# q of the first FFN tile loaded in runs of four tokens per partition

## The chip, the cores and the metric

The kernel runs on one core of one Trainium2 chip. The metric is the device time of one execution in microseconds (us). The engines are named as the profile names them: PE (TensorE, the matmuls), DVE (VectorE), ACT (ScalarE), POOL (GpSimd) and SP (SyncE). Repeated executions of one kernel mostly agree within 1% here, and each has a granted TensorE clock in its record (1.0 is full speed). A ratio is the mean time of one kernel's fast runs over that of the other's of the same rounds on the same chip, so it is not quite the ratio of the medians quoted beside it; the bracket behind it is its 95% interval.

## The reference

A recurrent attention (each head has a decay `gamma`) is followed by a gated FFN over all 3072 tokens:

```
B, H, S, D = 4, 8, 768, 64
gamma = 1.0 - 2.0 ** (-5.0 - np.arange(H))
for t in range(S):
    state = gamma * state + einsum('bhd,bhe->bhde', k[:, :, t], v[:, :, t])
    y[:, :, t] = (1 / sqrt(D)) * einsum('bhd,bhde->bhe', q[:, :, t], state)
x = y.transpose(0, 2, 1, 3).reshape(B * S, H * D)          # 3072 x 512
out = (sigmoid(x @ w_gate) * (x @ w_val)) @ w_out            # d_ff = 1536
```

## The kernel before

The tokens are cut into 24 chunks of 128, six for each batch, and into six FFN tiles of four chunks. An "up" group of the FFN computes 128 of the 1536 hidden columns of a tile (8 matmuls), a "down" group half the sum for 128 output rows (6 matmuls). The attention of tile t+1 is woven into the FFN of tile t. For each chunk, k and q are loaded, transposed on PE (chunks 0 to 11) and multiplied to scores; DVE masks these; PE adds the part inside the chunk ("intra") and the part from the state ("inter") in the PSUM tile `y`; DVE multiplies `y` by the decay table `taby` into the FFN's input `xT`. `y` has one buffer (pool `pa`, `bufs=1`), so a chunk's `y` starts only after the `xT` of the chunk before it.

Nearly all loads are issued by POOL (GpSimd), which also does some arithmetic. These are the parts, with cuts marked:

```python
    def load_kq(g):
        kn[g] = ld.tile([C, H, D], BF16, tag="kn", name="kn")
        qn[g] = ld.tile([C, H, D], BF16, tag="qn", name="qn")
        nc.gpsimd.dma_start(out=kn[g], in_=src(k, g))
        nc.gpsimd.dma_start(out=qn[g], in_=src(q, g))
    def load_chunk(g):
        load_kq(g)
        load_v(g, nc.gpsimd)
    ...
    def extend_taby():           # columns 384..767 = columns 0..383 times gamma^384
        nc.gpsimd.tensor_tensor(taby[:, :, 384:768], taby[:, :, 0:384],
                                gup.unsqueeze(2).to_broadcast([128, NP, 384]), op=ALU.mult)
    ...
    def y_out(g):
        c = g % NCH              # ... xT of chunk g reads columns c*128 .. of taby
        nc.vector.tensor_tensor(xT[g // 4][:, :, col:col + C], y[g], taby[:, :, c * C:(c + 1) * C], op=ALU.mult)
    ...
    keep_on(36)                  # 36 dummy matmuls
    transposes(0)
    make_taby(slice(256, 384))
    extend_taby()                # early
    ... load_gate_val(3..5), load_chunk(4), load_out(0..3), load_chunk(5..7)
    ... attention of chunks 0 to 3, with the first FFN groups of tile 0
    for t in range(NT):
        groups, steps, place = ups(t) + downs(t), [], []
        if t == 0:
            groups = groups[4:]
            steps = [lambda: step_t(4), lambda: step_s(4), lambda: step_y(4), lambda: step_t(5), lambda: step_s(5),
                     lambda: step_t(6), lambda: step_y(5, 6), lambda: step_t(7), lambda: step_y(6, 7)]
            place = [4, 5, 7, 9, 10, 11, 12, 13, 14]
        ...
        if t + 2 < NT:
            for g in range(4 * t + 8, 4 * t + 12):
                load_chunk(g)    # for t == 0: chunks 8 to 11, ahead of all groups of tile 0
        for i, group in enumerate(groups):
            ...
            group()
            for p, step in zip(place, steps):
                if p == i:
                    step()
```

## Time and profile before

| | before |
|---|---|
| median of 4 runs (range) | 240.16 us (239.56 to 241.09) |
| span of the profiled run | 238.1 us, PE busy 227.8 |
| FFN tile 0 / tile 1 entered by PE | 27.9 / 57.7 us |
| granted clock | 1.00 from its first record (6.0 us) on |

From the page of the kernel before come the PE row and the clock row (the span in 40 slices of about 6 us, each digit the tenths of a slice) and the engines' shares of the chain of work that ended last:

```profile
PE   7798999999999999999999999999999999999993
PEclk9999999999999999999999999999999999999999
...
PE 88%; POOL 6%; issue 2%; ACT 2%; DVE 1%; ACTq 0%; POOLq 0%; DVEq 0%
```

The rows have no hole after the fourth slice, and the chain is PE for 88% of the span. So any stretch in which PE waits is added to the time, and nothing that another engine saves shortens it unless PE waits for it.

### The profile page before, as it was taken

What the parts mean: (1) busy time and instruction counts of PE and PEld (TensorE: products, weight loads), DVE (VectorE), ACT (ScalarE), POOL (GpSimd) and SP (SyncE); (2) the same over time, 40 slices, a digit from 0 to 9 for tenths busy, and PEclk for the clock granted to TensorE, in tenths of its full rate; (3) what the DMA queues carried; (4) which work ended last, traced back from release to release, by engine and by line L of the source; (5) the groups of instructions that cost most, each with busy time, mean ns of one, the idle gap of its engine ahead of it and who ended that gap; (6) DMA issues with size and microseconds to landing.
All of it is one profiled execution on the core that took longest, in us unless ns stands there. A gap on an engine that the chain in (4) does not pass through costs nothing.

```text
span 238.1 us, 4313 instructions
## 1 busy us (share of the span) xinstructions
PE 227.8 (96%) x1716; PEld 118.9 (50%) x1742; DVE 102.0 (43%) x172; ACT 90.8 (38%) x169; POOL 95.9 (40%) x114
## 2 busy tenths in 40 slices
PE   7798999999999999999999999999999999999993
PEld 7565644555655554444554445444444554444441
DVE  3467446355545631256641346641346641243300
ACT  7764334425545431234333243223334321334221
POOL 8999874687889346994111001111000000000000
PEclk9999999999999999999999999999999999999999
DMA  7999999999999999999972361012100012100022
GB/s 131 192 189 188 195 205 200 189 212 230 233 169 139 92 138 163 263 175 156 159 110 88 91 104 29 3 45 89 47 0 0 3 44 88 47 0 0 0 88 88
DMA packets 77267, 27.27 MB, mean 115 GB/s; under 512 B 65024, under 2 KB 72704, under 8 KB 77248
## 3 DMA queue, kind: packets, MB, share of 16 engines
q0 software_dynamic: 57616, 16.78, 70.6%
q1 hardware_dynamic: 19632, 10.23, 21.6%
q8 instruction: 13, 0.21, 0.4%
q14 instruction: 6, 0.05, 0.1%
HBM read 28.31 MB, written 6.29 MB: 145 GB/s over the span
## 4 chain that ended last, share of the span: by engine, by line
PE 88%; POOL 6%; issue 2%; ACT 2%; DVE 1%; ACTq 0%; POOLq 0%; DVEq 0%
PE ff L250 49%; PE ff L281 26%; PE sA L168 3%; PE y L204 2%; PE z L190 2%; PE y L180 2%; PE tp L146 2%; POOL vs L158 1%; POOL kn L67 1%; POOL vf L62 1%; POOL qn L68 1%; ACT qkT L148 1%; PE ff L264 1%; ACT ob L286 1%; PE ff L293 1%
## 5 line engine op out<-in xcount | busy, mean ns | idle before, releaser
L255 DVE TENSOR_TENSOR hT<-gs,ff 128x512 bf16<-128x512 f32 (+1 forms) x72 | 48.6, 676 | 75.5 <-PE ff L250 73.9
L250 PE MATMUL ff<-xT,wg 128*128 128x512 bf16 (+1 forms) x276 | 71.5, 375 | 0.9 <-DVE xT L212 0.3
L250 PE MATMUL ff<-xT,wv 128*128 128x512 bf16 (+1 forms) x282 | 71.9, 375 | 0.4
L254 ACT ACTIVATE gs<-ff 128x512 f32<-128x512 f32 (+1 forms) x72 | 42.3, 588 | 68.8 <-PE ff L250 68.3
L281 PE MATMUL ff<-wo,hT 128*128 128x512 bf16 x280 | 65.0, 380 | 0.6 <-issue 0.2
L250 PEld LDWEIGHTS <-wv 128*128 128x128 bf16 x288 | 28.2, 98 | 32.7
L281 PEld LDWEIGHTS <-hT 128*128 128x128 bf16 x288 | 27.0, 98 | 31.6
L250 PEld LDWEIGHTS <-wg 128*128 128x128 bf16 x288 | 26.7, 98 | 30.2 <-issue 0.8
L158 POOL TENSOR_TENSOR vs<-vf,tabv 128x512 bf16<-128x512 f32 x18 | 18.6, 1048 | 47.1 <-PE y L204 42.1
L286 ACT COPY ob<-ff 128x512 f32<-128x512 f32 x24 | 14.0, 585 | 54.3 <-PE ff L281 49.1
L212 DVE TENSOR_TENSOR xT<-y,taby 128x512 bf16<-128x512 f32 x24 | 16.4, 685 | 20.1 <-PE y L204 20.0
L62 POOL DMA_DIRECT2D vf<-in_v_dram x23 | 20.7, 902 | 9.4 <-DMA kn<-in_k_dram 4.7
L173 DVE TENSOR_TENSOR stA<-sA,causal 128x512 bf16<-128x512 f32 x24 | 16.5, 687 | 18.6 <-PE sB L168 18.5
L67 POOL DMA_DIRECT2D kn<-in_k_dram x23 | 20.9, 907 | 7.0 <-DMA qn<-in_q_dram 4.4
L68 POOL DMA_DIRECT2D qn<-in_q_dram x23 | 20.4, 887 | 4.3 <-DMA wo<-in_moe_w_out_dram 2.3
L198 ACT CAST zbd<-z 64x256 bf16<-64x256 f32 x40 | 14.6, 366 | 13.6 <-PE z L190 13.2
L174 DVE TENSOR_TENSOR stB<-sB,causal 128x512 bf16<-128x512 f32 x24 | 16.3, 681 | 0.0
L148 ACT ACTIVATE qkT<-tp 128x1024 bf16<-128x1024 bf16 x12 | 12.3, 1024 | 5.1 <-PE tp L146 5.1
L293 PE MATMUL ff<-ident 128*128 128x128 bf16 x110 | 9.5, 251 | 2.6 <-POOL ident masks.py:199 1.6
L204 PE MATMUL y<-stA,vs 128*64 128x128 bf16 x96 | 9.7, 222 | 0.0
L293 PEld LDWEIGHTS <-ident 128*128 128x128 bf16 x110 | 8.0, 114 | 3.2 <-POOL ident masks.py:199 1.6
L204 PE MATMUL y<-stB,vs 128*64 128x128 bf16 x96 | 9.5, 221 | 0.0
(48 smaller groups left out, 112.9 us busy)
## 6 DMA issues: line engine op xcount, KB each, us to landing
out_dram<-ob SPq DMA_DIRECT2D x24, 256.0 KB, 2.0
vf<-in_v_dram POOLq DMA_DIRECT2D x23, 256.0 KB, 8.6
kn<-in_k_dram POOLq DMA_DIRECT2D x23, 128.0 KB, 8.4
qn<-in_q_dram POOLq DMA_DIRECT2D x23, 128.0 KB, 8.6
wg<-in_moe_w_gate_dram POOLq DMA_DIRECT2D x6, 256.0 KB, 5.8
wv<-in_moe_w_val_dram POOLq DMA_DIRECT2D x6, 256.0 KB, 6.6
wo<-in_moe_w_out_dram POOLq DMA_DIRECT2D x4, 384.0 KB, 11.0
kf<-in_k_dram SPq DMA_DIRECT2D x1, 256.0 KB, 3.4
```

Source lines behind the costliest of these rows:

```text
L62: eng.dma_start(out=vf[g], in_=src(v, g))
L67: nc.gpsimd.dma_start(out=kn[g], in_=src(k, g))
L68: nc.gpsimd.dma_start(out=qn[g], in_=src(q, g))
L158: eng.tensor_tensor(vs[g], vf[g], tabv[:, g % NCH, :].unsqueeze(2).to_broadcast([C, H, D]), op=ALU.mult)
L173: nc.vector.tensor_tensor(stA[g], sc[g][0], causal4, op=ALU.mult)
L204: nc.tensor.matmul(y[g][i * D:(i + 1) * D, p, :], vs[g][:, 2 * p + i, :], st[:, p, :], start=(first and p == 0), stop=True, skip_group_che ...
L212: nc.vector.tensor_tensor(xT[g // 4][:, :, col:col + C], y[g], taby[:, :, c * C:(c + 1) * C], op=ALU.mult)
L250: nc.tensor.matmul(u[:, lo:hi], w[:, kk, n1 * 128:(n1 + 1) * 128], xT[t][:, kk, lo:hi], start=(kk == 0), stop=(kk == KT - 1))
L254: nc.scalar.activation(gs[:, lo:hi], ps[0][:, lo:hi], AX.Sigmoid)
L255: nc.vector.tensor_tensor(hT[t][:, n1, lo:hi], gs[:, lo:hi], ps[1][:, lo:hi], op=ALU.mult)
L281: nc.tensor.matmul(o, hT[t][:, n1, sm * 128:(sm + 1) * 128], wo[:, n1, :], start=(n1 == 0), stop=(n1 == NFF - 1))
L293: nc.tensor.matmul(u[:, :128], ident, ident, start=True, stop=True)
```

## The change

The intent is to read q for the first tile (tokens 0 to 511) with one load instead of four. Each partition takes four consecutive tokens, so that the runs in memory are longer and there are fewer loads at the start. The tokens of a chunk of tile 0 are then in the order "j, p" (token 4p + j) through the mask, the decay table, the FFN and the stores, which put them in order again. The decay table of tile 0 becomes a table of its own (`taby0`). The table in plain order, `taby`, which chunk 4 and later chunks need, is now made from it during tile 0 by three ACT copies and one POOL multiply.

```diff
     def load_kq(g):
         kn[g] = ld.tile([C, H, D], BF16, tag="kn", name="kn")
-        qn[g] = ld.tile([C, H, D], BF16, tag="qn", name="qn")
         nc.gpsimd.dma_start(out=kn[g], in_=src(k, g))
-        nc.gpsimd.dma_start(out=qn[g], in_=src(q, g))
+        if g >= 4:
+            qn[g] = ld.tile([C, H, D], BF16, tag="qn", name="qn")
+            nc.gpsimd.dma_start(out=qn[g], in_=src(q, g))
...
-    nc.sync.dma_start(out=qf, in_=src(q, 0))
...
+    q0 = const.tile([128, H, 4 * D], BF16, name="q0")
+    nc.gpsimd.dma_start(out=q0, in_=q[0, :, 0:512, :].rearrange("h (p j) d -> p h (j d)", j=4))
...                                             # iota, mask and table of tile 0 in the order (j, p)
-    def extend_taby():
-        nc.gpsimd.tensor_tensor(taby[:, :, 384:768], taby[:, :, 0:384],
-                                gup.unsqueeze(2).to_broadcast([128, NP, 384]), op=ALU.mult)
+    def by_384(out, in_):
+        nc.gpsimd.tensor_tensor(out, in_, gup.unsqueeze(2).to_broadcast([128, NP, in_.shape[2]]), op=ALU.mult)
+    def taby_in_order(c):
+        nc.scalar.copy(taby[:, :, c * C:(c + 1) * C].rearrange("x n (p j) -> x n p j", j=4),
+                       taby0[:, :, c * C:(c + 1) * C].rearrange("x n (j p) -> x n p j", j=4))
...                                             # transposes_q0: 32 transposes of 64 columns, two copies
-    transposes(0)
-    make_taby(slice(256, 384))
-    extend_taby()
+    transposes_k(0)
+    keep_on(10)
+    transposes_q0()
+    make_taby0(slice(256, 384))
+    by_384(taby0[:, :, 384:512], taby0[:, :, 0:128])
...
-    transposes(3)
-    keep_on(16)
+    transposes_k(3)
...                                             # stores of tile 0: four of 64 KB for one of 256 KB
             place = [4, 5, 7, 9, 10, 11, 12, 13, 14]
+            steps += [lambda c=c: taby_in_order(c) for c in range(3)]
+            steps += [lambda: by_384(taby[:, :, 384:768], taby[:, :, 0:384])]
+            place += [0, 1, 2, 3]
```

More of the change, by code (lines that the diff above doesn't have):

```diff
@@ L89 @@
     kf = const.tile([C, H, D], F32, name="kf")
-    qf = const.tile([C, H, D], F32, name="qf")
     nc.sync.dma_start(out=kf, in_=src(k, 0))
-    nc.sync.dma_start(out=qf, in_=src(q, 0))
     nc.scalar.preload_act_table(AX.Exp)
     load_v(0, nc.sync)
+    q0 = const.tile([128, H, 4 * D], BF16, name="q0")
+    nc.gpsimd.dma_start(out=q0, in_=q[0, :, 0:512, :].rearrange("h (p j) d -> p h (j d)", j=4))
+    q0T = const.tile([128, NP, 4, 128], BF16, name="q0T")
     tokv = const.tile([128, NCH], I32, name="tokv")
@@ L99, with causal_mask @@
     toky = const.tile([128, 384], I32, name="toky")
-    nc.gpsimd.iota(toky, pattern=[[1, 384]], base=0, channel_multiplier=0)
+    nc.gpsimd.iota(toky, pattern=[[C, 3], [1, 4], [4, 32]], base=0, channel_multiplier=0)
     load_chunk(1)
-    causal = const.tile([128, 128], F32, name="causal")
-    nc.gpsimd.memset(causal, 1.0)
-    nc.gpsimd.affine_select(causal, causal, pattern=[[1, 128]], base=0, channel_multiplier=-1,
-                            compare_op=ALU.is_ge, fill=0.0)
+    def causal_mask(name, pattern):
+        m = const.tile([128, 128], F32, name=name)
+        nc.gpsimd.memset(m, 1.0)
+        nc.gpsimd.affine_select(m, m, pattern=pattern, base=0, channel_multiplier=-1,
+                                compare_op=ALU.is_ge, fill=0.0)
+        return m.unsqueeze(1).to_broadcast([128, NP, 128])
+    causal0 = causal_mask("causal0", [[1, 4], [4, 32]])
     load_chunk(2)
@@ L123, with make_taby0 @@
     taby = const.tile([128, NP, S], F32, name="taby")
-    def make_taby(cols):
+    taby0 = const.tile([128, NP, 512], F32, name="taby0")
+    def make_taby0(cols):
         for p in range(NP):
-            nc.scalar.activation(taby[:, p, cols], toky[:, cols], AX.Exp, scale=lgp[:, p:p + 1], bias=lsc)
-    def extend_taby():
-        nc.gpsimd.tensor_tensor(taby[:, :, 384:768], taby[:, :, 0:384],
-                                gup.unsqueeze(2).to_broadcast([128, NP, 384]), op=ALU.mult)
-    causal4 = causal.unsqueeze(1).to_broadcast([128, NP, 128])
+            nc.scalar.activation(taby0[:, p, cols], toky[:, cols], AX.Exp, scale=lgp[:, p:p + 1], bias=lsc)
+    def by_384(out, in_):
[3 more added lines that the diff above has]
+                       taby0[:, :, c * C:(c + 1) * C].rearrange("x n (j p) -> x n p j", j=4))
     xT, vs, qkT, sc, stA, stB, y = {}, {}, {}, {}, {}, {}, {}
@@ L140, in pair, with transposes_q0, transposes_k, q_of @@
         return t[:, 2 * p:2 * p + 2, :].rearrange("s h d -> s (h d)")
+    def transposes_q0():
+        for i in range(2):
+            tq = pf.tile([128, 2, 4, 128], BF16, tag="ff", name="tq")
+            for p in range(2):
+                for j in range(4):
+                    for k in range(2):
+                        nc.tensor.transpose(tq[k * D:(k + 1) * D, p, j, :],
+                                            q0[:, 2 * (2 * i + p) + k, j * D:(j + 1) * D], ident)
+            if i:
+                nc.vector.tensor_copy(q0T[:, 2:4], tq)
+            else:
+                nc.scalar.activation(q0T[:, 0:2], tq, AX.Copy)
+    def transposes_k(g):
+        tp = pa.tile([128, 2 * NP, C], BF16, tag="tp", name="tp")
+        for p in range(NP):
+            nc.tensor.transpose(tp[:, p, :], pair(kn[g], p), ident)
+        qkT[g] = at.tile([128, 2 * NP, C], BF16, tag="qkT", name="qkT", bufs=3)
+        nc.scalar.activation(qkT[g][:, 0:NP], tp[:, 0:NP], AX.Copy)
+    def q_of(g, rows, p):
+        if g < 4:
+            return q0T[rows, p, :, g * 32:(g + 1) * 32]
+        return qkT[g][rows, NP + p, :]
     def transposes(g):
@@ L167, in scores @@
                 half = slice(i * D, (i + 1) * D)
-                nc.tensor.matmul(sc[g][i][:, p, :], t[half, p, :], t[half, NP + p, :], start=True, stop=True)
+                nc.tensor.matmul(sc[g][i][:, p, :], t[half, p, :], q_of(g, half, p), start=True, stop=True)
     def masks(g):
@@ L172, in masks @@
         stB[g] = at.tile([128, NP, C], BF16, tag="stB", name="stB")
-        nc.vector.tensor_tensor(stA[g], sc[g][0], causal4, op=ALU.mult)
-        nc.vector.tensor_tensor(stB[g], sc[g][1], causal4, op=ALU.mult)
+        mask = causal0 if g < 4 else causal4
+        nc.vector.tensor_tensor(stA[g], sc[g][0], mask, op=ALU.mult)
+        nc.vector.tensor_tensor(stB[g], sc[g][1], mask, op=ALU.mult)
     def inter(g):
@@ L179, in inter @@
             for p in range(NP):
-                nc.tensor.matmul(y[g][:, p, :], zbd[(g - 1) % 2][:, p, :], qkT[g][:, NP + p, :],
+                nc.tensor.matmul(y[g][:, p, :], zbd[(g - 1) % 2][:, p, :], q_of(g, slice(0, 128), p),
                                  start=(p == 0), stop=False, skip_group_check=True)
@@ L211, in y_out @@
         col = (g % 4) * C
-        nc.vector.tensor_tensor(xT[g // 4][:, :, col:col + C], y[g], taby[:, :, c * C:(c + 1) * C], op=ALU.mult)
+        tab = taby0 if g < 4 else taby
+        nc.vector.tensor_tensor(xT[g // 4][:, :, col:col + C], y[g], tab[:, :, c * C:(c + 1) * C], op=ALU.mult)
     def step_t(g):
@@ L286, in down @@
         nc.scalar.copy(ob, o)
-        row = t * 512 + sm * 128
-        nc.sync.dma_start(out=out[row:row + 128, :], in_=ob)
+        rows = out[t * 512 + sm * 128:t * 512 + (sm + 1) * 128, :]
+        if t > 0:
+            nc.sync.dma_start(out=rows, in_=ob)
+        else:
+            for j in range(4):
+                nc.sync.dma_start(out=rows.rearrange("(p j) d -> j p d", j=4)[j], in_=ob[j * 32:(j + 1) * 32, :])
     def keep_on(n):
@@ L301 @@
     load_gate_val(2)
-    make_taby(slice(0, 256))
+    make_taby0(slice(0, 256))
     kn[0] = ld.tile([C, H, D], BF16, tag="kn", name="kn")
-    qn[0] = ld.tile([C, H, D], BF16, tag="qn", name="qn")
     nc.vector.tensor_copy(kn[0], kf)
-    nc.scalar.copy(qn[0], qf)
     keep_on(36)
-    transposes(0)
-    make_taby(slice(256, 384))
-    extend_taby()
+    transposes_k(0)
[3 more added lines that the diff above has]
+    by_384(taby0[:, :, 384:512], taby0[:, :, 0:128])
     for s in range(3, NFF // 2):
         load_gate_val(s)
+    causal4 = causal_mask("causal", [[1, 128]])
     load_chunk(4)
@@ L321 @@
     keep_on(8)
-    transposes(1)
+    transposes_k(1)
     inter(0)
@@ L334 @@
     state_out(1)
-    transposes(2)
+    transposes_k(2)
     nc.scalar.preload_act_table(AX.Sigmoid)
```

## The prediction

> **What bounds the kernel now.** I read the page first, then the waits, then the timelines of PE, DVE and POOL between 10 and 72 us, then the DMA issues with their times to landing. The page says that PE is the bound:
>
> ```profile
> PE 227.8 (96%) x1716; PEld 118.9 (50%) x1742; DVE 102.0 (43%) x172; ACT 90.8 (38%) x169; POOL 95.9 (40%) x114
> ...
> DMA  7999999999999999999972361012100012100022
> ...
> L67 POOL DMA_DIRECT2D kn<-in_k_dram x23 | 20.9, 907 | 7.0 <-DMA qn<-in_q_dram 4.4
> ```
>
> PE is busy 227.8 of 238.1 us, so it idles only 10.3 us in all, 5 us of which is before 25 us. The early PE time is partly dummy work (`keep_on`, 110 matmuls, 9.5 us in its row). After 25 us PE runs without a gap worth naming. The DMA row is 9 up to slice 21, about 130 us: behind the PE the load queue is full for the first half. Every load of k, q, v and weights is issued by POOL, and POOL does so in program order, 0.9 us each. Next, POOL's timeline:
>
> ```profile
> 36.72 0.87 POOL L68 DMA_DIRECT2D qn<-in_q_dram  x1 [0.75 <-DMA wo<-in_moe_w_out_dram]
> 39.23 0.89 POOL L62 DMA_DIRECT2D vf<-in_v_dram  x1 [1.64 <-DMA wo<-in_moe_w_out_dram]
> ...
> 44.29 0.90 POOL L62 DMA_DIRECT2D vf<-in_v_dram  x1
> 45.17 0.90 POOL L67 DMA_DIRECT2D kn<-in_k_dram  x1
> ...
> 56.69 0.89 POOL L62 DMA_DIRECT2D vf<-in_v_dram  x1 [0.55 <-DVE stA L173]
> ```
>
> This is the view the prediction rests on. Program order puts the twelve loads of chunks 8 to 11 at the head of FFN tile 0, which PE enters at 27.9 us, yet POOL starts them at 45.17 and issues the last (v of chunk 11) at 56.69. It is held back: I put each issue beside the landing of the issue eight before it. The first `wo` was issued at 27.05 and took 9.4 us to land, at 36.44; the eighth issue after it, q of chunk 6, starts at 36.72. Over all 77 POOL issues from the ninth on, no issue starts less than 0.28 us after the landing eight back, and many start exactly then. So **at most eight loads are in flight**, and POOL moves at the pace of the DMA landings.
>
> Where PE and DVE are meanwhile:
>
> ```profile
> 43.51 0.69 DVE L212 TENSOR_TENSOR xT<-y,taby 128x512 bf16<-128x512 f32 x1
> ```
> ```profile
> 51.21 0.39 PE L180 MATMUL y<-qkT,zbd 128*128 128x128 bf16 x4
> ...
> 57.72 0.81 PE L250 MATMUL ff<-xT,wg 128*128 128x384 bf16 x4
> ```
>
> DVE makes xT of chunk 4 at 43.51, PE starts y of chunk 5 at 51.21, and tile 1 of the FFN starts at 57.72. The table that the first of these reads is extended by one POOL multiply, early:
>
> ```profile
> L130 POOL TENSOR_TENSOR taby<-taby,gup x1: 2825/2825/2825, 17.3 to 17.3; 128x1536 f32<-128x1536 f32 x1
> ```
>
> [...] POOL runs in program order throughout, for instance four v scalings only at 70.35, after the last load of chunk 15. [...] the scaling of v for chunk 3 took 2.18 us instead of 0.68, while the table multiply ran from 17.27 to 20.10. [...] The window 20 to 30 us, nearly all 512 B packets, moves 194 GB/s; the k/q/v mix at 44 to 49 us, mostly smaller packets, 180 GB/s: a small difference here. [...]
>
> **The change part by part.** *Loads.* Removed: one q load on SP and three on POOL. Each k or q load lands about 0.9 us after the one before it in the full queue, that of SP about 1.06, so 3 x 0.9 + 1.06 = 3.8 us of queue time go. Added: one q0 load. It writes 524 kB in 512 B packets like the weights', at 194 GB/s: 2.7 us. Net 1.1 us less queue time, and two POOL issues less (1.8 us). POOL also does 512 instead of 1536 columns of the early table multiply: 2.83 x 512/1536 = 0.94 us, saving 1.9 us.
>
> *Start.* q0 is first in POOL's queue but is four loads in one; sharing the engines with k and v of chunk 0 I estimate landing near 7.8 us, against 5.30 for q of chunk 0 before. Then 32 small transposes (about 1 us at the 0.03 us that the 64-column matmuls of L204 are apart), and two copies, of which ACT's costs 1.02 us like L148's. The scores of chunk 0 move from 7.51 to about 10.2, and the first FFN matmul from 16.98 to about 19.4. Against that, the k copies of chunks 1 to 3 are half as long; v of chunk 3 lands earlier and no longer meets the multiply on DVE, so PE's 1.4 us of waiting between 19.8 and 21.2 and the 16 dummy matmuls (1 us) go. Entering tile 0, I expect PE about 1 us later than before (-1 to +2).
>
> *The table.* The columns 384 to 767 of `taby` now come from three ACT copies (0.6 us each, ACT has room) and then one POOL multiply of 1536 columns, placed after group 3 of tile 0. In POOL's FIFO that is **behind the twelve loads of chunks 8 to 11**. xT of chunk 4 reads columns 512 to 639, so it can't run at 43.5 any more. The last of the twelve waits for k of chunk 9 to land (before: issued 48.17, 8.0 us to landing, 56.1). After the change that is earlier by the 1.1 us, and by some 0.5 us because the third store of tile 0 is not yet competing: 54.5. So: 54.5 + 0.3 (wake) + 0.9 (issue) + 2.83 (multiply) = 58.5 us.
>
> *What stands behind it.* DVE is blocked from about 44 to 58.5. PE goes on through the down groups (ACT empties them) until y of chunk 5, which needs the single y buffer, near 52. At 58.5 DVE must do, in order: xT of chunk 4 (0.69), scaling v of 5 (0.68), two masks of 5 (1.37): 61.3. Only then can PE do scores of 6, state and intra of 5: to 62.2, where before it was at 52.21: +10.0. Then down group (1.3), transposes, down group, step of 6, down group, masks of 7 and xT of 6, as before: 67.9 against 57.72. **The stall is about +10.2 us.** The start's +1 us is hidden in it, since PE waits for POOL anyway. From 57.72 on, 180.4 us of nearly pure PE work follow unchanged; the two small waits at 62.6 and 71.3 (0.4 us) may go, as loads are then far ahead. During the 6 us gap the clock may drop; [...] at a chance of 65% that is +1.3. Sum: 240.15 + 10.2 + 1.3 - 0.4 = 251.25, rounded to 251.
>
> *Stores.* Tile 0's four stores become sixteen of 64 KB; SP is idle then and the packets stay 2 KB. No effect on the path.
>
> **The rivals.** *A: only the start counts*, as if the multiply were not late: -1.5 to +2 us, so 239 to 242. For it: the author surely meant the multiply to be hidden behind tile 0, with 12 groups in front of its reader. Against: the POOL timeline above, since the reader comes at 43.5 and POOL is at chunk 7 then. *B: the start gains*: fewer POOL issues free the scaling of v of chunk 1, which released PE at 11.76, and the DVE block at 18.47 goes: about 237. Against: q0's late landing. *C: POOL gets ahead.* If only its own issue time of 0.88 us counted, the multiply would end near 49 (k of chunk 4 at about 21 us, then 23 loads and 4 of weights, 24 us, and 2.8), before y of chunk 5 at 51.2, and no stall would show: as A. Against: eight in flight, and landings shift only by 1 to 2 us. *D: stall and a cold clock in full*, or a worse chain behind it: 253 to 255.
>
> **Range and chances.** The end of the multiply is uncertain by 1.5 us, the DVE-PE chain behind it by 1, the clock by 2: 247.5 to 254.5. The mark for slower by over 2% is 244.95; only A, B or C fall short of it. Faster 0.04, same 0.07, slower 0.89.
>
> **What would show it.** Right: in the changed profile DVE's xT of chunk 4 starts near 58.5 with a wait of over 10 us released by the POOL multiply; that multiply follows v of chunk 11 on POOL; PE has a gap of 5 to 7 us before y of chunk 5; tile 1 starts near 68; a PEclk digit below 9 after the gap for the clock step; scores of chunk 0 near 10 us for the start. Wrong: the multiply ending before 52, or PE busy through 50 to 60. If q0 lands by 6 us, the start's term is wrong but the sum stands.

## The result and the profile after

The changed kernel took 252.91 us (median of 4, 252.54 to 253.33), against 240.16 for the kernel before. The ratio is 1.0528 [1.0489, 1.0567]: slower by 5%. The result is correct. The page of the changed kernel, in the rows shown above for before:

```profile
span 251.0 us, 4356 instructions
...
PE 230.2 (92%) x1726; PEld 120.0 (48%) x1752; DVE 100.9 (40%) x173; ACT 92.5 (37%) x172; POOL 95.8 (38%) x115
...
PE   4898999931999999999999999999999999999994
...
PEclk9999999995699999999999999999999999999999
DMA  7999999999999999279999245101210002200022
...
PE 71%; DMA 15%; POOL 7%; issue 3%; DVE 1%; ACT 1%; POOLq 0%; ACTq 0%; DVEq 0%
```

PE's busy time is nearly the same, 230.2 for 227.8 us, while the span grew by 12.9. The PE row shows where: slices 9 and 10 (counted from 1; 50 to 63 us) read 3 and 1. The clock row reads 5 and 6 in slices 10 and 11. The chain now consists of DMA for 15% of the span, which had none before: the end of the program hangs on loads. The waits say on what (engine, line, what it waited for, total us, times, longest):

```profile
DVE xT L248 <- POOL taby L138: 15.8, 1, 15.8
...
PE y L215 <- DVE xT L248: 8.7, 1, 8.7
```

The next three views are the timelines of POOL, DVE and PE of the changed kernel (start, duration, engine, line, operation, and in brackets the idle time before it and what ended it):

```profile
56.98 0.89 POOL L62 DMA_DIRECT2D vf<-in_v_dram  x1 [1.05 <-DMA kn<-in_k_dram]
57.88 2.76 POOL L138 TENSOR_TENSOR taby<-taby,gup 128x1536 f32<-128x1536 f32 x1
```
```profile
44.21 0.69 DVE L291 TENSOR_TENSOR hT<-gs,ff 128x512 bf16<-128x512 f32 x1 [1.04 <-PE ff L286]
60.68 0.69 DVE L248 TENSOR_TENSOR xT<-y,taby 128x512 bf16<-128x512 f32 x1 [15.78 <-POOL taby L138]
```
```profile
51.25 1.46 PE L317 MATMUL ff<-wo,hT 128*128 128x512 bf16 x5
61.43 0.58 PE L215 MATMUL y<-qkT,zbd 128*128 128x128 bf16 x4 [8.72 <-DVE xT L248]
...
64.30 2.65 PE L317 MATMUL ff<-wo,hT 128*128 128x512 bf16 x6
...
71.00 0.81 PE L286 MATMUL ff<-xT,wg 128*128 128x384 bf16 x4
```

Read them from top to bottom. POOL issues v of chunk 11, the last of the twelve loads of chunks 8 to 11, at 56.98, after k of chunk 9 has landed. Only then does it multiply the table, from 57.88 to 60.64. DVE has stood idle since 44.9, since xT of chunk 4 reads columns 512 to 639 of that table. PE went on with down groups until 52.7 and then had nothing to do until DVE had emptied `y`. The down group at 64.30 took 2.65 us for six matmuls, against 1.46 us for the five recorded at 51.25: that is the half clock, which this trace shows (granted 0.50) from 56.5 to 66.7 us. Tile 1 starts at 71.00, 13.3 us later than the 57.72 of before. From there to the end it is 180.0 us, against 180.4 before. So the whole loss lies before 71 us.

### The profile page after: what moved, and what is told of

It reads as the page before. It is cut to its first block, busy times and chain, and to the rows that moved or that the text cites. A ratio compares the mean times of both kernels' runs of the same rounds, so it can differ in the third digit from the quotient of the medians.

```text
span 251.0 us, 4356 instructions
## 1 busy us (share of the span) xinstructions
PE 230.2 (92%) x1726; PEld 120.0 (48%) x1752; DVE 100.9 (40%) x173; ACT 92.5 (37%) x172; POOL 95.8 (38%) x115
## 3 DMA queue, kind: packets, MB, share of 16 engines
HBM read 28.31 MB, written 6.29 MB: 138 GB/s over the span
## 4 chain that ended last, share of the span: by engine, by line
PE 71%; DMA 15%; POOL 7%; issue 3%; DVE 1%; ACT 1%; POOLq 0%; ACTq 0%; DVEq 0%
PE ff L286 41%; PE ff L317 22%; DMA wo<-in_moe_w_out_dram 4%; DMA wg<-in_moe_w_gate_dram 4%; DMA kn<-in_k_dram 3%; DMA vf<-in_v_dram 3%; PE sA L202 2%; PE y L239 2%; POOL taby L138 2%; PE y L215 1%; PE z L225 1%; POOL wg L82 1%; POOL wv L82 1%; POOL kn L66 1%; PE tp L180 1%
## 5 line engine op out<-in xcount | busy, mean ns | idle before, releaser
L317 PE MATMUL ff<-wo,hT 128*128 128x512 bf16 x280 | 66.1, 384 | 0.6 <-issue 0.2
L208 DVE TENSOR_TENSOR stA<-sA,causal 128x512 bf16<-128x512 f32 x24 | 16.5, 686 | 13.3 <-PE sB L202 13.2
L69 POOL DMA_DIRECT2D qn<-in_q_dram x20 | 18.2, 911 | 3.3 <-DMA wo<-in_moe_w_out_dram 1.7
L233 ACT CAST zbd<-z 64x256 bf16<-64x256 f32 x40 | 14.7, 367 | 12.9 <-PE z L225 12.5
L215 PEld LDWEIGHTS <-zbd 128*128 128x128 bf16 x80 | 6.1, 99 | 13.0 <-issue 9.0
L215 PE MATMUL y<-qkT,zbd 128*128 128x128 bf16 x28 | 2.9, 230 | 8.7 <-DVE xT L248 8.7
L239 PE MATMUL y<-stA,vs 128*64 128x128 bf16 x96 | 10.3, 226 | 0.0
```

What stands on the lines that cost most here:

```text
L208: nc.vector.tensor_tensor(stA[g], sc[g][0], mask, op=ALU.mult)
L239: nc.tensor.matmul(y[g][i * D:(i + 1) * D, p, :], vs[g][:, 2 * p + i, :], st[:, p, :], start=(first and p == 0), stop=True, skip_group_che ...
L317: nc.tensor.matmul(o, hT[t][:, n1, sm * 128:(sm + 1) * 128], wo[:, n1, :], start=(n1 == 0), stop=(n1 == NFF - 1))
```

## The experiments

The theory is that of the prediction: the multiply's place in POOL's program order, behind twelve loads, is the whole loss. The rivals are that the new layout (strided copies, small stores, late start) costs part of it, and that the clock, not the wait, is the main term. Twelve kernels were run. The expectations count them by label: "the first experiment" is the next one below, "the fifth" the first under "What the start is worth", "the eighth" the first there that starts from the changed kernel.

### The twelve loads behind the multiply

The changed kernel, with nothing altered but the order in which POOL gets its work:

```diff
-            place += [0, 1, 2, 3]
+            steps += [lambda g=g: load_chunk(g) for g in range(8, 12)]
+            place += [0, 1, 2, 3, 3, 3, 3, 3]
...
-        if t + 2 < NT:
+        if 0 < t < NT - 2:
             for g in range(4 * t + 8, 4 * t + 12):
                 load_chunk(g)
```

> The changed kernel, with the twelve loads of chunks 8 to 11 issued after the late table multiply instead of ahead of it. Nothing else differs. Theory (the whole loss is the multiply's place behind twelve loads in POOL's order): the multiply ends near 48 us instead of 60.6, PE's gap before y of chunk 5 is gone, the granted clock is 1.00 throughout, tile 1 starts near 59 instead of 71.0, time 241.5 (240.5 to 242.5). What stays against the kernel before is the later start, 29.25 instead of 27.9 us into tile 0. Rival (the loss lies in the new q layout, the sixteen small stores or the load queue): stays above 248.

It took 240.48 us (240.17 to 240.94) beside 240.60 for the kernel before: ratio 0.9996 [0.9966, 1.0025]. Its POOL, DVE and PE timelines:

```profile
45.17 2.76 POOL L138 TENSOR_TENSOR taby<-taby,gup 128x1536 f32<-128x1536 f32 x1
```
```profile
47.96 0.69 DVE L248 TENSOR_TENSOR xT<-y,taby 128x512 bf16<-128x512 f32 x1 [3.62 <-POOL taby L138]
```
```profile
51.99 0.39 PE L215 MATMUL y<-qkT,zbd 128*128 128x128 bf16 x4
```

The multiply is the same instruction, 12.7 us earlier. DVE still waits 3.6 us for it, but PE comes to y of chunk 5 without a wait. The whole 5% is gone, with the new layout, the copies, the sixteen small stores and the later start all in place. The time is just below the range that was expected, since the later start cost nothing here. So the place of the multiply is **necessary** for the loss, and everything else in the change, taken together, moves the time by nothing measurable (-0.3 to +0.3%). That its parts cost nothing each does not follow; the start is taken up again below.

### Only the multiply late, in the kernel before

The reverse: the kernel before, with none of the new layout, but with the columns that chunks 4 and 5 read multiplied at the place where the change does it. Columns 384 to 511 are still made early, as chunk 3 reads them.

```diff
-    extend_taby()
+    extend_taby(0, 128)
...
             place = [4, 5, 7, 9, 10, 11, 12, 13, 14]
+            steps += [lambda: extend_taby(128, 384)]
+            place += [3]
```

> The kernel before, with only one thing of the change: columns 512 to 767 of the table are multiplied on POOL after group 3 of tile 0, behind the loads of chunks 8 to 11 (columns 384 to 511 stay early). No q0, no new stores. Theory: the multiply takes 1.9 us and ends near 59.5, xT of chunk 4 waits for it, the clock drops to 0.5 in the gap, time 251.5 (250 to 253). Rival (the new start or layout costs the time): within 1 us of 240.2, or faster since the start loses the collision on DVE at 18.5.

It took 252.82 us (252.72 to 252.97) beside 240.60: 1.0507 [1.0479, 1.0536], the loss of the change. Its POOL and PE timelines show the same picture:

```profile
57.52 1.91 POOL L130 TENSOR_TENSOR taby<-taby,gup 128x1024 f32<-128x1024 f32 x1
```
```profile
60.20 0.59 PE L180 MATMUL y<-qkT,zbd 128*128 128x128 bf16 x4 [9.67 <-DVE xT L212]
```

The late multiply is also **sufficient**. The rivals that put part of the loss on the layout are out, to within the noise of some 0.3%.

### Six loads ahead, six behind

If POOL's queue is the cause, half the loads should give about half the loss.

```diff
-            place += [0, 1, 2, 3]
+            steps += [lambda g=g: load_chunk(g) for g in range(10, 12)]
+            place += [0, 1, 2, 3, 3, 3]
...
-            for g in range(4 * t + 8, 4 * t + 12):
+            for g in range(4 * t + 8, 4 * t + (12 if t else 10)):
```

> The changed kernel with six loads ahead of the late multiply (chunks 8 and 9) and six behind it (10 and 11). Theory: the multiply starts right after v of chunk 9, near 50.9 us, and ends near 53.7; PE's gap shrinks to about 2 us[...]; tile 1 starts near 63, time 244.9 (244 to 246). Rival (the wait is for the ACT copies or the landing of data, not for POOL's place): no change from 252.9; rival (any late multiply above some place costs the same): near 252.

It took 246.58 us (245.00 to 247.26) beside 240.60: 1.0226 [1.0176, 1.0276], a loss of 6.0 us for half the loads. The dose is right: the multiply starts at 51.30, between 45.17 with none ahead and 57.88 with twelve. The size was missed by 1.7 us, at least in part because the expected time left out a fall of the clock, which was an assumption of mine that no run had shown. PE's timeline and its windows (span in us, busy time and count for PE, PEld, DVE, ACT and POOL, then granted clock, DMA share, GB/s):

```profile
54.85 0.38 PE L215 MATMUL y<-qkT,zbd 128*128 128x128 bf16 x4 [1.99 <-DVE xT L248]
```
```profile
54.00:58.00 4.00, 2.00 (x21) 1.25 (x21) 3.90 (x7) 0.00 (x0) 4.00 (x6) 0.71 1.77 249
58.00:62.00 4.00, 4.00 (x17) 1.94 (x16) 1.67 (x3) 1.16 (x2) 4.00 (x6) 0.50 1.98 200
```

The clock was 0.50 from 55.7 to 62.5 us. It fell 0.9 us after the gap of 2 us had ended; in the 3.4 us before the fall PE was busy for 0.94 us. So the gap of 2 us is part of the 2.5 us in which PE stood idle there; the rest belongs to the next wait, of 0.82 us, which the small attention matmuls had for DVE's mask. The last section sets all falls of the clock side by side.

### Dummy matmuls in the gap

To part the wait from the clock, 140 dummy matmuls were put before y of chunk 5 in the changed kernel. They are to fill the gap; nothing else is edited.

```diff
+            steps.insert(6, lambda: keep_on(140))
+            place.insert(6, 12)
```

> The changed kernel, with 140 dummy matmuls (about 7.8 us) put in front of y of chunk 5, where PE waits for the late multiply. They end before the wait does. Theory that the halved clock is part of the loss: the granted clock stays 1.00, the down group that took 2.65 us takes 1.46 again, time 251.8, 1.1 us less than the changed kernel (0.6 to 1.6). Rival (DVE's queue sets the pace there, so the clock costs nothing): same as the changed kernel, 252.9 within 0.4.

The four executions fell into two groups: 253.39 and 253.46 us with a granted clock of 0.993, and 250.71 and 250.46 with 1.000 (before: 240.60). The profiled one was of the slower group. In its windows the clock held through the gap and fell after it:

```profile
62.00:64.00 2.00, 0.60 (x5) 0.39 (x5) 2.00 (x5) 0.00 (x0) 2.00 (x3) 0.98 1.42 175
64.00:66.00 2.00, 1.91 (x17) 0.99 (x17) 2.00 (x5) 0.00 (x0) 2.00 (x4) 0.50 1.85 169
```

From 62 to 64 us PE was busy 0.6 of 2 us, while DVE worked off its backlog without a pause. So this run didn't keep PE warm throughout, and as a test of the sum it is inconclusive. The clock is not the only difference between the two groups either: they are 2.8 us apart, while the half clock in this trace (granted 0.50) lasted 3.41 us and so cost at most half of that. In the same trace the multiply came 0.9 us later than in the changed kernel (57.88):

```profile
58.75 2.76 POOL L138 TENSOR_TENSOR taby<-taby,gup 128x1536 f32<-128x1536 f32 x1
```

The other group has no trace. The run was repeated with dummies in both places:

```diff
         inter(g)
+        if g == 5:
+            keep_on(25)
...
+            steps.insert(6, lambda: keep_on(150))
+            place.insert(6, 12)
```

> The changed kernel with 150 dummy matmuls ahead of y of chunk 5 and 25 more between y of chunk 5 and the scores of chunk 6, so that PE is never idle for longer than about a microsecond in the stall. In the earlier run with 140 dummies the executions fell in two groups: clock 1.000 at 250.5 and 250.7 us, clock 0.993 at 253.4 and 253.5. Theory: now all have clock 1.000 and 250.6 us (250.2 to 251.2); the stall alone is then 10.2 us and the clock the remaining 2.3. Rival (the two groups have another cause, such as where the loads land): both groups still there at clock 1.000.

All four executions had a clock of 1.000 and took 251.12 us (250.89 to 251.27) beside 240.40: 1.0443 [1.0420, 1.0466]. In its trace the multiply and the y of chunk 5 come when they do in the changed kernel (57.88 and 61.43):

```profile
57.94 2.76 POOL L138 TENSOR_TENSOR taby<-taby,gup 128x1536 f32<-128x1536 f32 x1
```
```profile
61.48 0.38 PE L215 MATMUL y<-qkT,zbd 128*128 128x128 bf16 x4 [0.59 <-DVE xT L248]
```

So the wait alone costs 251.12 - 240.40 = 10.7 us. The clock costs the rest: (252.91 - 240.16) - 10.7 = 2.0 us. The two warm executions of the run before would give 10.0 and 2.8. The wait is the main term either way, and the clock a sixth to a fifth of the loss.

### What the start is worth

The changed kernel gains nothing from its saved loads even where the multiply is early. Two more groups of runs ask why. In the kernel before, the scaling of v of chunk 3 on DVE (at 18.47) took 2.18 us while the table multiply ran on POOL (17.27 to 20.10), and the one at 13.62, of the same shape, took 0.68. So first, a start without this overlap, made from the kernel **before**: the part of the table for chunks 4 and 5 is multiplied after the loads of `wo`, and the dummy matmuls at `transposes(3)` are dropped.

```diff
-    extend_taby()
+    extend_taby(0, 128)
...
         load_out(s)
+    extend_taby(128, 384)
...
-    up(0, 1, 0, 384)
     transposes(3)
-    keep_on(16)
+    up(0, 1, 0, 384)
```

> The kernel before, without the new layout: columns 512 to 767 of the table are multiplied on POOL right after the loads of w_out, ahead of the twelve loads, so that the multiply no longer meets the scaling of v of chunk 3 on DVE; the transposes of chunk 3 go between the first two up groups and the 16 dummy matmuls after them are dropped. Theory: the scaling of v of chunk 3 takes 0.68 instead of 2.18 us, scores of chunk 3 start near 20.1 instead of 22.16, tile 0 and everything after it come 2.1 us earlier, 238.3 us (237.8 to 239.3). Rival (the later waits absorb it, the loads being the limit): within 0.5 us of 240.5.

It took 240.49 us (239.36 to 242.84) beside 240.40: 0.9999 [0.9970, 1.0027], a miss. The scaling of v of chunk 3 (at 19.07) took 0.69 us, with the two parts of the multiply at 17.34 to 18.45 and 32.02 to 33.93. PE entered tile 0 at 25.9, 2 us earlier as intended. PE's and POOL's timelines around 70 us show where that went, in the slowest of the six executions (242.84 us), which is the profiled one:

```profile
72.82 0.32 PE L190 MATMUL z<-vs,kn 128*64 128x64 bf16 x8 [3.27 <-POOL vs L158]
```
```profile
70.81 0.89 POOL L62 DMA_DIRECT2D vf<-in_v_dram  x1
71.71 4.04 POOL L158 TENSOR_TENSOR vs<-vf,tabv 128x512 bf16<-128x512 f32 x4
```

PE came to the state of chunk 8 at 69.5 and waited 3.3 us, and after the wait the clock was 0.50 from 73.9 to 77.3 us, which the median execution (2.4 us faster) need not share. The scaling of v of chunk 8 is POOL's from that chunk on, and it stands behind the loads of chunks 12 to 15. It is the disease of the late multiply again. In the kernel before, PE reaches this point just as POOL does:

```profile
71.47 0.32 PE L190 MATMUL z<-vs,kn 128*64 128x64 bf16 x8 [0.15 <-POOL vs L158]
```

So what is saved at the start can be lost again there. The test is to take that scaling off POOL as well:

```diff
-        scale_v(g, nc.vector if g < 8 else nc.gpsimd)
+        scale_v(g, nc.vector if g < 12 else nc.gpsimd)
```

> The tuned kernel before (the fifth experiment), with the scaling of v of chunks 8 to 11 on DVE instead of POOL. There PE reached tile 0 two microseconds earlier and then lost 3.3 us at 69.5 us, waiting for the scaling of v of chunk 8, which stood behind the loads of chunk 15 in POOL's order. Theory (the same kind of wait as the late multiply's): the wait goes, the early gain stays, 238.4 us (237.9 to 239.2), clock 1.000. Rival (the load queue itself is late, so the next step waits for k or v of chunk 8 to 11 to land instead): within 0.7 us of 240.4.

```profile
69.52 0.32 PE L190 MATMUL z<-vs,kn 128*64 128x64 bf16 x8
```

The wait is gone, and with it the time comes to 238.17 us (237.52 to 239.06) beside 240.57: 0.9898 [0.9867, 0.9930]. This is the fastest kernel. That the DVE scaling would gain little without the earlier start is argued from the wait of 0.15 us in the kernel before; no run has it alone. The tuned kernel beats both the kernel before and the changed one, the first by 1%.

The same two steps for the changed kernel with its loads behind the multiply, first `transposes_k(3)` between the two up groups alone:

```diff
     up(0, 0, 0, 384)
-    up(0, 1, 0, 384)
     transposes_k(3)
+    up(0, 1, 0, 384)
```

> The kernel of the first experiment, with the transposes of k of chunk 3 between the first two up groups instead of after them, so that ACT's copy is done when the scores of chunk 3 come. Theory: the 0.9 us gap of PE ahead of those scores goes, 239.7 us (239.2 to 240.3), a little faster than the kernel before but slower than the tuned kernel before. Rival (masks and the next wait absorb it): same as the first experiment, 240.5.

It took 239.94 us (239.84 to 240.77) beside 240.40: 0.9989 [0.9968, 1.0010]. Then with v of chunks 8 to 11 scaled on DVE too:

```diff
-        scale_v(g, nc.vector if g < 8 else nc.gpsimd)
+        scale_v(g, nc.vector if g < 12 else nc.gpsimd)
```

> The changed kernel with the twelve loads behind the multiply, the transposes of chunk 3 moved forward (the eighth experiment), and the scaling of v of chunks 8 to 11 on DVE. Theory: PE is not ahead of POOL here, so nothing waits and nothing is gained: 239.9 (239.4 to 240.4), and slower than the tuned kernel before with the same step on DVE, since its start is later. Rival (POOL's load was holding something else back): below 239.3.

It took 239.54 us (238.55 to 240.06) beside 240.57: 0.9951 [0.9923, 0.9979]. That is 1.4 us more than the kernel before with the same two steps. What is left is, as far as the traces tell, the start of the new layout: PE enters tile 0 at 27.10 here and at 25.88 there. (The two profiled executions, 238.55 and 238.91 us, don't show the difference of the medians; the second lost 0.89 us at 97.3 waiting for ACT.) The last three runs take the start apart. They begin with a load of a quarter of q0, the rest being set to zero, in the kernel with the loads behind the multiply:

```diff
-    nc.gpsimd.dma_start(out=q0, in_=q[0, :, 0:512, :].rearrange("h (p j) d -> p h (j d)", j=4))
+    nc.vector.memset(q0[:, :, D:4 * D], 0.0)
+    nc.gpsimd.dma_start(out=q0[:, :, 0:D], in_=q[0, :, 0:128, :].rearrange("h p d -> p h d"))
```

> The kernel of the first experiment (twelve loads behind the multiply), with a q0 load of a quarter of the size: 256-byte reads of the first 128 tokens only, the rest of the tile set to zero by DVE. The result is wrong on purpose. Theory (the start of the change is later because q0's four-fold load lands late, 9.35 us): q0 lands near 6.5, the transposes of q0 follow the dummies at 8.1 without a wait, scores of chunk 0 start near 9.8 instead of 11.1, the first up group starts near 17.9, time 239.2 (238.5 to 240). Rival (the 32 transposes and the two copies cost the time, or the dummies before them): within 0.4 us of the first experiment's 240.5.

It took 239.85 us (239.50 to 240.19) beside 240.40: 0.9975 [0.9952, 0.9998]. The time is inside the range of the theory, but the theory's steps are not what happened: q0 landed at 5.90, but its transposes started only at 8.65, and the first up matmul came at 19.09, where 17.9 was expected, against 19.26 with the full load. PE had been held up by something else: its dummy matmuls start at 3.21, since the identity they multiply is made on POOL after q0's issue. Then the quarter load with the identity made first, and v of chunks 8 to 11 on DVE:

```diff
+    ident = const.tile([128, 128], BF16, name="ident")
+    make_identity(nc, ident)
     q0 = const.tile([128, H, 4 * D], BF16, name="q0")
...
-    ident = const.tile([128, 128], BF16, name="ident")
-    make_identity(nc, ident)
...
-        scale_v(g, nc.vector if g < 8 else nc.gpsimd)
+        scale_v(g, nc.vector if g < 12 else nc.gpsimd)
```

> The kernel with the quarter-size q0 load (wrong result on purpose), with the identity made on POOL ahead of that load's issue, and the scaling of v of chunks 8 to 11 on DVE. Theory (the changed start has two gates: q0's landing, and PE's dummies that can start only at 3.21 instead of 1.60 us because the identity comes after q0's issue): the dummies start near 2.0, scores of chunk 0 near 8.7 instead of 10.4, the first up group near 17.4 instead of 19.1, time 238.5 (237.8 to 239.3). Rival (the chain of scores, masks and copies sets the start): first up group stays near 19.

It took 238.42 us (237.76 to 239.76) beside 240.57: 0.9916 [0.9874, 0.9957]. The dummies start at 1.43, q0's transposes at 6.29, and the first up matmul at 16.97, as in the kernel before (16.98). These are the first up matmuls of the kernel before, of the quarter load, and of the quarter load with the identity first:

```profile
16.98 0.81 PE L250 MATMUL ff<-xT,wg 128*128 128x384 bf16 x4 [0.30 <-DVE xT L212]
```
```profile
19.09 0.81 PE L287 MATMUL ff<-xT,wg 128*128 128x384 bf16 x4 [0.30 <-DVE xT L249]
```
```profile
16.97 0.81 PE L287 MATMUL ff<-xT,wg 128*128 128x384 bf16 x4 [0.30 <-DVE xT L249]
```

Last, the identity first, but the full and correct q0 load, in the kernel with its loads behind the multiply, the tuned start and v of chunks 8 to 11 scaled on DVE:

```diff
+    ident = const.tile([128, 128], BF16, name="ident")
+    make_identity(nc, ident)
     q0 = const.tile([128, H, 4 * D], BF16, name="q0")
     nc.gpsimd.dma_start(out=q0, in_=q[0, :, 0:512, :].rearrange("h (p j) d -> p h (j d)", j=4))
...
-    ident = const.tile([128, 128], BF16, name="ident")
-    make_identity(nc, ident)
```

> The run with the loads of chunks 8 to 11 behind the multiply, v of chunks 8 to 11 scaled on DVE and the tuned start (239.54 us), with the identity now made before q0's issue and the full q0 load: one of the two gates of the start opened, the other (q0's landing) left. If the identity's place is what counts, the dummy matmuls begin near 1.4 us instead of 3.2, the first up matmul comes near 17.0 as with the quarter load, and the time is near 238.4. If q0's landing is the gate that remains, the q0 transposes still start near 8 to 9.4 us, the first up matmul stays at 18 to 19, and the time is 239.3 (range 238.6 to 240.0). I expect the second.

It took 241.40 us (239.77 to 241.61) beside 240.37: 1.0020 [0.9990, 1.0051]. The first up matmul came at 21.33. Both theories missed the time. The second was right about the gate (the transposes start at 9.10) and missed the first up matmul by over 2 us. PE's timeline:

```profile
5.17 0.72 PE L333 MATMUL ff<-ident 128*128 128x128 bf16 x10
9.10 1.92 PE L157 MATMUL tq<-ident,q 128*64 128x128 bf16 x32 [3.20 <-DMA q<-in_q_dram]
```

The dummies start 1.8 us earlier and are used up 3.2 us before q0 lands. The clock halves meanwhile: it is 0.50 from 8.0 to 14.9 us, and the transposes take 1.92 us instead of 1.08. No run fills this gap with more dummies. So the new start has **two gates in a row**, the identity behind q0's issue and q0's landing. Opening the second without the first brought the first up matmul forward by 0.2 us (quarter load), opening the first without the second made it later, and only both together reach the start of the kernel before. The second gate was opened with a load that computes a wrong result, and that also takes three quarters of q0's bytes off the queue, which no run separates.

## Why the prediction was right

The mechanism was right: the multiply stands behind twelve loads, DVE and then PE wait for it, and the clock falls in the gap. One step of it did not come, the saving of 1.6 us in the load queue. The time was 1.9 us (0.8%) above the predicted 251.0, and it was not luck that it came so near: the two large errors, the multiply's end and the clock, have the same sign. Point by point:

- **The multiply's end, 58.5 us.** It was 60.64, so this term was 2.1 us too small. The multiply itself is as expected (2.76 us), but the last load was issued at 56.98 instead of 54.8. The saving of 1.1 us of queue time and of 0.5 us for a later store, both estimates, did not arrive: k of chunk 9 landed at 56.43, hardly different from the 56.14 of before. The trace shows the queue less well filled at the start: q0 took 8.0 us to land (9.35 us), POOL stood 1.46 us waiting for v of chunk 1, and v of chunk 3 landed at 18.76, against 18.45 before. The last `wo` landed at 42.71 in both kernels. That the lost fill is what ate the saving is argued from these times; no run isolates it.
- **q0's landing, 7.8 us.** It came at 9.35 in this trace. It also varies: in the profiled runs with this load unaltered the transposes that need it started between 7.99 and 9.92 us. An estimate that gives it one value is too narrow.
- **The stall, +10.2 us, less 0.4 regained later: net 9.8.** 10.7 net was measured with the clock held, 0.9 more (span against span of the two profiled executions, 249.4 and 238.1, it is 11.3, 1.5 more). The cause is the later multiply. The net is off by less than the multiply's 2.1 us; 0.3 of the difference is DVE's chain, in which xT, scaling and two masks took 2.5 us (60.68 to 63.17), where 2.8 was put down. The rest is not accounted for; the executions of the kernel before alone spread over 1.5 us.
- **PE's gap, 5 to 7 us.** It was 8.72, from the later multiply.
- **The clock, +1.3 us in the sum (2 us at a chance of 65%, an estimate).** It fell in every execution (0.97 to 0.98 over the span; in the profiled one it was 0.50 for 10.24 us) and cost about 2.0 us. The size was right and the chance too low. With the drop taken as certain the predicted sum would have been 251.95; the 1.0 us still missing is the stall's term above.
- **The start, about +1 us, hidden.** PE entered tile 0 at 29.25 instead of 27.9, +1.35. That it is hidden was right. There is a reason that the prediction didn't see as well: even without the stall, PE and POOL meet at the scaling of v of chunk 8, as the runs with a faster start showed. One of the "two small waits" that the prediction wrote off, the one at 71.3, is the visible part of this balance.
- **Smaller points.** The ACT copies that put the table in order took 1.09 us each, not 0.6; they end by 35.4 us, far ahead of the multiply. The sixteen stores show no cost, as said. Some sums and readings of the working are slightly off, and nothing hangs on them: the k, q and v of chunk 0 are loaded by SP, not POOL; PE idles 4.4 us before 25 us, not 5; from 62.2 on "as before" gives 67.7, not 67.9, so a stall of 10.0; and the terms of rival C add up to 47.8, not 49. The clock record in the trace of the kernel before begins only at 6.04 us; the 36 dummy matmuls ahead of it start 0.107 us apart, and those after it 0.055 us.
- **The rivals.** A (only the start counts, 239 to 242) describes what is left once the multiply is moved: 240.48 us. B (the start gains, about 237) does not: the new start is no gain in any run. C (POOL gets ahead) needed POOL's own issue time to be the limit. In the trace after, as before, no issue of POOL starts less than 0.28 us after the landing of the issue eight back, over 75 issues. The semaphore fields of the trace, which the views don't print, say where the eight comes from: POOL's loads use eight semaphores in turn, each of the 75 issues takes the one that the issue eight back used, and 61 of them have the wait for it recorded (73 of 77 in the kernel before). So the eight is in the program as it was built. Whether the chip has a limit of its own is not shown.

One also sees how the multiply's place could look harmless: in program order many groups of PE work stand between it and its reader. But in POOL's own order twelve loads stood in front of it, and they went at the pace of the landings: the last was issued at 56.98, 0.55 us after k of chunk 9 had landed.

## What to carry to other kernels

Before moving an instruction to an engine that also issues loads, look at where that engine **is** in time when the reader comes, not at how many groups of other work stand between. Here the multiply started at 57.88 us behind the twelve loads and at 45.17 ahead of them. Moving the loads behind the instruction cost nothing measurable here, and it gave back the whole 5%. And before working on a faster start, look for a later place where the bounding engine meets another one with almost no slack (a wait of 0.15 us in the kernel before). Here a start 2 us earlier gained nothing (240.49 beside 240.40 us, with a wait of 3.3 us at that place in the profiled execution) until the place was opened as well (238.17).

## What the traces show of the clock, a load and a copy

- The clock fell after a gap of 1.99 us with sparse work behind it (six loads ahead), and after a gap of 1.23 us with PE busy 0.6 of the next 2 us (140 dummies). Every stretch at one clock value that a trace records from beginning to end lasted a whole number of 3.41 us windows (14 at full and then 3 at half clock in the changed kernel). Counted in these windows, the six falls in mid-kernel came after windows with 0 (the changed kernel), 0 (only the multiply late), 0.94 (six loads ahead), 1.05 (the start tuned from the kernel before), 1.15 (140 dummies) and 1.28 us (the identity first with the full q0) of PE work. In the traces of the kernel before and of the changed kernel, the clock stayed up after every window with 2.39 us or more. So in these runs the falls go with little work in a window, not with the longest gap alone; no run varies the work of a window by itself, and what happens between 1.28 and 2.39 us is not shown here.
- The load of q0 (524 kB written) took 8.0 us beside the other loads in flight, and the quarter of it 4.6. No run here loads q0 with nothing else in flight.
- An ACT copy with rearranged columns, 128x512 f32, took 1.09 us, against 0.59 us for the plain copy of that shape from PSUM. The two also differ in their source, which no run here separates.
